# Attention, two-stage routing and a feed-forward network in one kernel: new ranks for the last blocks of attention, and more comparisons by differences

## The chip, the cores and the metric

The kernel runs on one core of a Trainium2 chip. The metric is the device time of one execution in microseconds. One execution was profiled; every row below is of it.

## The reference

Three layers follow one another. Attention over 2 x 8 heads of 768 positions (a window of 128 positions and 4 sink positions) gives a row of 512 numbers for each of 1536 tokens. A gate of 8 experts then assigns the tokens greedily, best logit first, 192 tokens to an expert, and each expert applies two products to its tokens. A last network with a sloped ReLU follows.

```
scores = np.where(is_sink | in_window, scale * q @ k.T, -1e9)
x = softmax(scores) @ v                    # 1536 x 512 after the heads are joined
logits = x @ w_gate                        # 1536 x 8
for idx in np.argsort(-logits.flatten()):  # the best logit first
    tok, e = idx // E, idx % E
    if assigned[tok] >= 0 or counts[e] >= cap: continue
    assigned[tok] = e; counts[e] += 1
out[mask_e] = maximum(x[mask_e] @ w1[e], 0) @ w2[e]
h = out @ w_in
return (maximum(h, 0) + alpha * minimum(h, 0)) @ w_out
```

## The kernel before

Attention runs over 12 blocks of 128 tokens, numbered 0 to 11 in the order of the work, each in four steps of two heads. TensorE forms scores (L459) and transposes the exponentials (L494); VectorE masks and takes minima (L469) and forms the low halves `ptl` of the transposed exponentials (L504); ScalarE takes exponentials (L480) and the high halves `pth` (L503). TensorE then weights the values (L545 to L553) into a bank `pv` of PSUM. A block fills two such banks, one for each half of its heads, and there are two of them in all, so that a block's first bank is that of the block before.

`fin` normalises one half of a block: three VectorE instructions `r` (L575), its reciprocal (L577) and `x` (L572), the last of which frees the bank. `send` stores the block's `x` and brings it to the gate: blocks 0 to 9 through a transposing DMA, blocks 10 and 11 through TensorE (L590), a high half on ScalarE (L593) and a low half on VectorE (L595), both called `xT`. The gate's product (L619) and a copy (L625) give the logits `L`. Twice, at blocks 1 and 5, VectorE also prepares the sinks' values (`vsh`, L432).

The first phase of the routing (`closing(0, ...)`) then compares each token's best logit with those of all others. It does so in two groups, blocks 0 to 8 and blocks 9 to 11: the maxima `m` of the group's tokens (L953), their row `mrow` on all partitions (TensorE L981, ScalarE L985), and for each block c1 a matrix `cm` of comparisons, whose columns TensorE counts (L1047). A comparison has two forms: directly on VectorE (L1000, from 32-bit `mrow`), or "via" a difference `minus` on ScalarE or GpSimd (L1005, L1007), of which VectorE takes the sign from 16-bit numbers (L1011 for the diagonal, L1015 for the sides). Comparisons of a block with blocks of its own group went via differences; those of blocks 0 to 8 with the 384 columns of blocks 9 to 11 went directly, nine instructions at L1000. After all counts the phase ends (L1059 on), and expert 0's tokens are gathered.

The order is set by a planner, `Plan.run`. Every `task` has an engine or a choice of two, an assumed duration, and what it reads and writes. A task's rank is the length of the longest chain behind it plus its `boost`. The planner plays the program with the assumed durations; where several tasks could start within 0.03 us on an engine, the one of highest rank goes. On the chip each engine executes its list in that order. Attention and the first phase's comparisons are planned together, the rest afterwards.

Of the kernel before, what the change touches and what calls it, by code (L numbers as in the profile page):

```python
# [212 lines left out]
OP = mybir.AluOpType  # L213
# [3 lines left out]
B, H, S, D = 2, 8, 768, 64  # L217
NB = S // 128
NBLK = B * NB
# [5 lines left out]
TURNED = 2  # L225
URGENT = 10.0
EAGER = 40.0
ORDER = "k q a b w s c d"
BY_ACT = (0, 1, 3)
BIG = 1.0e30  # L230
# [7 lines left out]
def dve(n):  # L238
    return n / 960 + 0.065
# [6 lines left out]
def attention(tc, nc, plan, ctx, qT, kT, v, vs, wg, xd, x_blocks, L, l_blocks, n_sink, window, ident, identr):  # L246
# [6 lines left out]
    task = plan.task  # L253
# [24 lines left out]
    vsh_res, sv_res = [Res() for _ in range(B)], [Res() for _ in range(B)]  # L278
# [73 lines left out]
    svf, isv = [None] * B, [None] * B  # L352
# [210 lines left out]
    def fin(t, hf):  # L563
        bank, r = PV[t, hf], r_r.new()
        b = t // NB
        if hf == 0:
            X[t] = r_x.new()
        x = X[t]
        o = lambda: bank.tile[:, 0:HC].rearrange("p (h c) -> p h c", c=D + 1)

        def scale():
            nc.vector.tensor_tensor(x.tile[:, hf * 256:(hf + 1) * 256].rearrange("p (h d) -> p h d", h=4), o()[:, :, 0:D],  # L572
                                    r.tile.unsqueeze(2).to_broadcast([128, 4, D]), OP.mult)

        task({"DVE": 0.13}, lambda: nc.vector.tensor_scalar(r.tile, o()[:, :, D], 1.0e-9, svf[b], OP.add, OP.mult),  # L575
             r=[bank.part("o"), sv_res[b]], w=[r])
        task({"DVE": 0.1}, lambda: nc.vector.reciprocal(r.tile, r.tile), w=[r])  # L577
        task({"DVE": dve(256)}, scale, r=[bank.part("o"), r], w=[x.part(hf)])

    def send(t):  # L580
        b, x = t // NB, X[t]
        parts = [x.part(0), x.part(1)]
        task({"SP": 0.06}, lambda: nc.sync.dma_start(out=xd[block(t) * 128:(block(t) + 1) * 128, :], in_=x.tile), r=parts,
             w=[x_blocks[t]], nbytes=1 << 18)
        if t >= NBLK - TURNED:
            pt, xT = r_pt.new(), r_xT.new()

            def turn():
                for c in range(NP):
                    nc.tensor.transpose(pt.tile[:, c], x.tile[:, c * 128:(c + 1) * 128], ident)  # L590

            pe(0.5, turn, parts, [pt])
            task({"ACT": act(DM)}, lambda: nc.scalar.activation(xT.tile[:, 0], pt.tile, AF.Copy, scale=svf[b]),  # L593
                 r=[pt, sv_res[b]], w=[xT.part(0)])
            task({"DVE": dve(DM) + 0.065}, lambda: nc.vector.scalar_tensor_tensor(  # L595
                xT.tile[:, 1], pt.tile, svf[b], xT.tile[:, 0], OP.mult, OP.subtract), r=[pt, sv_res[b], xT.part(0)],
                w=[xT.part(1)])
            XT[t] = xT
            return
        x16, xs, xT = r_x16.new(), r_xs.new(), r_xT.new()  # L600
        task({"ACT": 0.613}, lambda: nc.scalar.activation(x16.tile[:, 0], x.tile, AF.Copy, scale=svf[b]),
             r=[*parts, sv_res[b]], w=[x16.part(0)])
        task({"POOL": 0.67}, lambda: nc.gpsimd.tensor_scalar(xs.tile, x.tile, svf[b], 0.0, OP.mult, OP.add),
             r=[*parts, sv_res[b]], w=[xs])
        task({"POOL": 1.12}, lambda: nc.gpsimd.tensor_tensor(x16.tile[:, 1], xs.tile, x16.tile[:, 0], OP.subtract),
             r=[xs, x16.part(0)], w=[x16.part(1)])
# [230 lines left out]
class Routed:  # L837
# [94 lines left out]
    def closing(self, s, st, groups, r_bank, hold=(), fetched=False):  # L932
# [15 lines left out]
        for a, b in groups:  # L948
# [41 lines left out]
            for a1, b1 in done:  # L990
                for c1 in range(a1, b1):
                    cm, cut = self.r_cm.new(), []
                    at = c1 * 128
# [21 lines left out]
                        nc.vector.tensor_scalar(d, d, 0.0, None, OP.is_gt if op is OP.is_lt else OP.is_ge)  # L1015

                    lo = 0 if a1 == a else a
                    via = a1 == a and (c1 * 7 % 12) < self.VIA[s]
                    rr = [m.part(a1), *(rows if a1 == a else fresh)]
                    if a1 == a:  # L1020
                        sides = ((0, at, at + 128, None), (1, 0, at, OP.is_lt), (2, at + 128, b * 128, OP.is_le))
                    else:
                        sides = ((2, a * 128, b * 128, OP.is_le),)
                    if via:
                        for x, y, kk in ((0, at + 128, (0, 1)), (at + 128, b * 128, (2,))):
                            if y > x:
                                n = y - x
                                seq.append(task({"ACT": act_sb(n), "POOL": n * 1.0e-3 + 0.02},
                                                lambda e, x=x, y=y, f=minus: f(e, x, y), r=rr, bias=self.EVEN,
                                                w=[cm.part(k) for k in kk if k != 1 or at]))  # L1030
# [571 lines left out]
```

## Time and profile before

| | |
|---|---|
| median of 3 runs | 682.1 us (680.96 to 685.27) |
| time of the profiled execution | 686.03 us |
| its span, first to last instruction | 684.3 us |

The span and the time of the profiled execution differ by 1.7 us, which lies around the instructions. The profiled execution is 3.9 us above the median of the three runs. A span of one execution is thus to be compared with that of another, and the median with a median.

### The profile page before, as it was taken

Reading aid. Unit: us, or ns where it says so; the run is one execution under the profiler, and the core shown is the slowest. Engines: PE = TensorE matmul, PEld = TensorE weight load, DVE = VectorE, ACT = ScalarE, POOL = GpSimd, SP = SyncE. Lnnn points to the kernel's source line nnn. Section 1 sums busy time; section 2 is a strip of 40 time slices with the busy share of each in tenths; the row PEclk is TensorE's granted clock in tenths of the full one; section 3 lists DMA queues with packets and bytes.
Section 4 is the critical chain, followed back from the end, with each engine's and each line's share of the span. In section 5 each row is a group of like instructions: output and inputs, shape, how many; then the busy total and the mean of one; then the engine's idle time right before and its main releaser. Section 6 shows DMA issues by size and latency. Waiting matters only on the chain.

```text
span 684.3 us, 12642 instructions
## 1 busy us (share of the span) xinstructions
PE 605.0 (88%) x4490; PEld 519.1 (76%) x4491; DVE 505.5 (74%) x1203; ACT 394.6 (58%) x835; POOL 399.2 (58%) x415
## 2 busy tenths in 40 slices
PE   6789994789789695998899999989899999999996
PEld 3566773479788584778888878788798888889995
DVE  6799989789499899797888577777845556874430
ACT  6588896254474556246774344467555447766552
POOL 4766735344354477267766565667556556766663
PEclk9999996589899898799999999999999999999999
DMA  7756332536773444025610004257000326610001
GB/s 241 225 142 138 94 94 83 188 113 227 253 276 97 165 138 147 1 63 181 201 65 2 2 24 139 62 185 233 23 0 1 116 61 185 200 33 1 0 1 46
DMA packets 40283, 76.10 MB, mean 111 GB/s; under 512 B 15518, under 2 KB 22204, under 8 KB 40124
## 3 DMA queue, kind: packets, MB, share of 16 engines
q1 hardware_dynamic: 37916, 68.45, 32.6%
q0 software_dynamic: 2304, 6.84, 2.9%
q8 instruction: 35, 0.57, 0.3%
q14 instruction: 28, 0.23, 0.1%
HBM read 66.30 MB, written 6.36 MB: 106 GB/s over the span
## 4 chain that ended last, share of the span: by engine, by line
PE 49%; DVE 28%; issue 7%; DMA 7%; ACT 5%; POOL 3%; SPq 1%; POOLq 0%; DVEq 0%; ACTq 0%
PE h L1453 15%; PE o L1474 14%; DVE cm L1000 4%; PE s L459 4%; PE h L1378 3%; PE pt L494 3%; DVE ohs L1147 2%; DVE w L799 2%; DVE spl L1321 2%; DMA raw<-w 2%; PE h L1385 2%; PE r L1296 2%; ACT spl L1330 2%; DMA xg<-xd,sidx 2%; POOL spl L1321 2%
## 5 line engine op out<-in xcount | busy, mean ns | idle before, releaser
L1321 POOL TENSOR_TENSOR spl<-w,spl 128x512 fp32r<-128x512 f32 x106 | 141.3, 1335 | 98.4 <-ACT spl L1330 96.2
L1474 PE MATMUL o<-spl,gt 128*128 128x512 f32 x576 | 152.6, 407 | 1.0 <-POOL gt L1321 1.0
L1453 PE MATMUL h<-x,spl 128*128 128x384 f32 x768 | 149.7, 345 | 1.3 <-POOL x L1321 0.7
L1453 PEld LDWEIGHTS h<-x,spl 128*128 128x128 f32 x768 | 138.7, 193 | 6.7 <-DVE x L1321 1.1
L1474 PEld LDWEIGHTS o<-spl,gt 128*128 128x128 f32 x576 | 107.0, 193 | 21.1 <-POOL gt L1321 1.9
L1321 POOL TENSOR_TENSOR spl<-raw,spl 128x512 fp32r<-128x512 f32 x57 | 75.8, 1336 | 36.7 <-ACT spl L1330 27.5
L1330 ACT CAST spl<-w 128x512 fp32r<-128x512 f32 x128 | 78.6, 615 | 29.4 <-PE o L1474 22.2
L1459 DVE SCALAR_TENSOR_TENSOR v<-h,way,t 128x384 f32<-128x384 f32 x64 | 39.0, 611 | 58.6 <-ACT t L1457 58.4
L1457 ACT ACTIVATE t<-h,slope 128x384 f32<-128x384 f32 x64 | 37.0, 579 | 73.1 <-PE h L1453 73.1
L1378 PE MATMUL h<-xT,spl 128*128 128x384 f32 x192 | 59.0, 372 | 8.8 <-DVE jt L1366 8.8
L1330 ACT CAST spl<-raw 128x512 fp32r<-128x512 f32 x94 | 56.4, 619 | 16.8 <-PE o L1474 10.4
L1378 PE MATMUL h<-h,spl 128*128 128x384 f32 x192 | 56.1, 362 | 2.5 <-DVE jt L1366 2.5
L1461 ACT CAST gt<-v 128x384 fp32r<-128x384 f32 x64 | 32.8, 513 | 39.2 <-DVE v L1459 37.7
L1321 DVE TENSOR_TENSOR gt<-v,gt 128x384 fp32r<-128x384 f32 x41 | 38.6, 942 | 20.3 <-ACT gt L1461 20.3
L1047 PEld LDWEIGHTS <-cm 128*128 128x128 bf16 x684 | 24.2, 99 | 37.8 <-DVE cm L1000 27.7
L1000 DVE TENSOR_SCALAR cm<-mrow,m 128x384 bf16<-128x384 f32 (+10 forms) x85 | 51.9, 647 | 1.1 <-ACT mrow L985 1.1
L1321 DVE TENSOR_TENSOR spl<-raw,spl 128x512 fp32r<-128x512 f32 x39 | 40.7, 1050 | 14.4 <-ACT spl L1330 14.2
L1380 PE MATMUL h<-xT,spl 128*128 128x192 f32 x192 | 48.8, 254 | 0.0
L480 ACT ACTIVATE P<-sm,mn 128x260 f32<-128x260 f32 (+1 forms) x96 | 43.2, 490 | 9.6 <-DVE mn L469 8.7
L1380 PE MATMUL h<-h,spl 128*128 128x192 f32 x192 | 48.1, 251 | 0.0
L1378 PEld LDWEIGHTS h<-xT,spl 128*128 128x128 f32 x192 | 37.0, 193 | 11.7 <-DVE jt L1366 10.3
L806 POOL TENSOR_TENSOR w<-w,sg 128x512 f32<-128x512 f32 x18 | 22.2, 1234 | 39.4 <-DVE w L799 26.2
(219 smaller groups left out, 1307.8 us busy)
## 6 DMA issues: line engine op xcount, KB each, us to landing
raw<-w SPq DMA_DIRECT2D x64, 512.0 KB, 3.9
r<-w_in SPq DMA_DIRECT2D x16, 512.0 KB, 3.6
r<-w_out SPq DMA_DIRECT2D x16, 512.0 KB, 4.0
vraw<-v SPq DMA_DIRECT2D x4, 768.0 KB, 11.6
xd<-x SPq DMA_DIRECT2D x12, 256.0 KB, 2.0
k<-kT SPq DMA_DIRECT2D x11, 260.0 KB, 5.4
q<-qT SPq DMA_DIRECT2D x11, 256.0 KB, 2.8
mrow<-md SPq DMA_DIRECT2D x3, 384.0 KB
```

What stands on the lines that cost most here:

```text
L459: nc.tensor.matmul(s.tile[:, :n], lhsT=qs[t].tile[half, p], rhs=kk, start=True, stop=True)
L480: task({"ACT": act(n) + 0.137}, lambda h=h, sm=sm, mn=mn: nc.scalar.activation(P[t].tile[:, h, :n], sm.tile[:, :n], AF.Exp, bias=mn.tile, ...
L1000: nc.vector.tensor_scalar(cm.tile[:, x:y], mrow[:, x:y], m.tile[:, c1:c1 + 1], None, op)
L1321: eng.tensor_tensor(*aps(), OP.subtract)
L1330: (nc.scalar.copy if e == "ACT" else nc.vector.tensor_copy)(b.tile[:, 0], get())
L1378: nc.tensor.matmul(ps.tile[:, 0:2 * CAP], lhsT=w[:, 0, k], rhs=x.rearrange("p a t -> p (a t)"), start=first and k == 0, stop=False, skip_g ...
L1380: nc.tensor.matmul(ps.tile[:, CAP:2 * CAP], lhsT=w[:, 1, k], rhs=x[:, 0], start=False, stop=last and k == len(xs) - 1, skip_group_check=True)
L1453: nc.tensor.matmul(ps.tile[:, 0:CH], lhsT=w[:, i, k], rhs=x[:, j], start=(k == n == 0), stop=(k == KD - 1 and n == 2))
L1457: task({"ACT": act(CH)}, lambda: nc.scalar.activation(t.tile, ps.tile[:, 0:CH], AF.Copy, scale=slope), r=[ps, weights.way_res], w=[t])
L1459: task({"DVE": dve(CH) + 0.065}, lambda: nc.vector.scalar_tensor_tensor(v.tile, ps.tile[:, 0:CH], way, t.tile, OP.mult, OP.max), r=[ps, t, ...
L1461: task({"ACT": act_sb(CH)}, lambda: nc.scalar.copy(gt.tile[:, 0], v.tile), r=[v], w=[gt.part(0)])
L1474: nc.tensor.matmul(ops[t].tile, lhsT=gt.tile[:, i, sl], rhs=wo.tile[:, j], start=(f == n == 0), stop=(f == FB - 1 and n == 2))
```

## The change

Three things change. The three instructions of `fin` get longer assumed durations (0.2, 0.17 and 0.42 in place of 0.13, 0.1 and 0.33), in all blocks. In the last three blocks `fin` gets a boost of 40, as do the two halves `xT` of blocks 10 and 11. And of the nine comparisons of blocks 0 to 8 with blocks 9 to 11, those with c1 % 3 other than 2 (six of them) go via differences.

```diff
+LAST = 3
@@ fin
+        up = EAGER if t >= NBLK - LAST else 0.0
-        task({"DVE": 0.13}, lambda: nc.vector.tensor_scalar(r.tile, o()[:, :, D], 1.0e-9, svf[b], OP.add, OP.mult),
-             r=[bank.part("o"), sv_res[b]], w=[r])
-        task({"DVE": 0.1}, lambda: nc.vector.reciprocal(r.tile, r.tile), w=[r])
-        task({"DVE": dve(256)}, scale, r=[bank.part("o"), r], w=[x.part(hf)])
+        task({"DVE": 0.2}, lambda: nc.vector.tensor_scalar(r.tile, o()[:, :, D], 1.0e-9, svf[b], OP.add, OP.mult),
+             r=[bank.part("o"), sv_res[b]], w=[r], boost=up)
+        task({"DVE": 0.17}, lambda: nc.vector.reciprocal(r.tile, r.tile), w=[r], boost=up)
+        task({"DVE": 0.42}, scale, r=[bank.part("o"), r], w=[x.part(hf)], boost=up)
@@ send
-                 r=[pt, sv_res[b]], w=[xT.part(0)])
+                 r=[pt, sv_res[b]], w=[xT.part(0)], boost=EAGER)
-                w=[xT.part(1)])
+                w=[xT.part(1)], boost=EAGER)
@@ closing
-                    via = a1 == a and (c1 * 7 % 12) < self.VIA[s]
+                    via = (a1 == a or c1 % 3 != 2) and (c1 * 7 % 12) < self.VIA[s]
-                        for x, y, kk in ((0, at + 128, (0, 1)), (at + 128, b * 128, (2,))):
+                        for x, y, kk in ((0, at + 128, (0, 1)), (at + 128, b * 128, (2,))) if a1 == a else (
+                                (a * 128, b * 128, (2,)),):
```

The lines of the changed kernel stand one to three further down (L572 becomes L573, L595 L597, L1000 L1002, L1007 L1009, L1015 L1017). All instructions keep their number but for these six comparisons, each of which becomes a difference and a sign. From the end of the first phase on, every engine's order is the one of before.

The first place is VectorE at block 11, where the block's two halves `x` stand among the comparisons of the first group. Before:

```order
L572 TENSOR_TENSOR x_2357<-pv_2296,r_2346 128x256
L1015 TENSOR_SCALAR cm_2317<-cm_2317 128x1024
L504 TENSOR_TENSOR ptl_2367<-pt_2342,pth_2359 128x256
L595 SCALAR_TENSOR_TENSOR xT_2363<-pt_2307,scv_163,xT_2363 128x512
L575 TENSOR_SCALAR r_2392<-pv_2348,scv_163 128x4
L1015 TENSOR_SCALAR cm_2331<-cm_2331 128x896
L577 RECIPROCAL r_2392<-r_2392 128x4
L1011 TENSOR_TENSOR cm_2361<-cm_2361,trih 128x128
L572 TENSOR_TENSOR x_2357<-pv_2348,r_2392 128x256
```

After, at the same place:

```order
L573 TENSOR_TENSOR x_2347<-pv_2294,r_2322 128x256
L577 TENSOR_SCALAR r_2357<-pv_2339,scv_163 128x4
L1017 TENSOR_SCALAR cm_2324<-cm_2324 128x1024
L579 RECIPROCAL r_2357<-r_2357 128x4
L597 SCALAR_TENSOR_TENSOR xT_2355<-pt_2330,scv_163,xT_2355 128x512
L573 TENSOR_TENSOR x_2347<-pv_2339,r_2357 128x256
L1013 TENSOR_TENSOR cm_2327<-cm_2327,trih 128x128
L1017 TENSOR_SCALAR cm_2327<-cm_2327 128x128
L1017 TENSOR_SCALAR cm_2327<-cm_2327 128x896
```

The second half of block 11 now leaves ahead of four signs that stood before it (two diagonals, 128 and 896 columns). Its `xT`, further on, and the maxima of the second group have the same place in VectorE's list as before, behind the same comparisons.

The second place is the second group, on GpSimd. Before, its differences after the last three of the first group:

```order
L1007 TENSOR_SCALAR cm_2433<-mrow,m_2265 128x256
L1007 TENSOR_SCALAR cm_2438<-mrow,m_2265 128x1024
L1007 TENSOR_SCALAR cm_2467<-mrow,m_2265 128x1152
L1007 TENSOR_SCALAR cm_2555<-mrow,m_2265 128x256
L1007 TENSOR_SCALAR cm_2560<-mrow,m_2265 128x1408
L1283 DMA xg_2819<-xd,sidx_2812 128x512
```

After:

```order
L1009 TENSOR_SCALAR cm_2423<-mrow,m_2252 128x256
L1009 TENSOR_SCALAR cm_2436<-mrow,m_2252 128x1024
L1009 TENSOR_SCALAR cm_2436<-mrow,m_2252 128x128
L1009 TENSOR_SCALAR cm_2557<-mrow,m_2252 128x384
L1009 TENSOR_SCALAR cm_2565<-mrow,m_2252 128x384
L1009 TENSOR_SCALAR cm_2573<-mrow,m_2252 128x384
L1009 TENSOR_SCALAR cm_2583<-mrow,m_2252 128x256
L1009 TENSOR_SCALAR cm_2595<-mrow,m_2252 128x1408
L1286 DMA xg_2825<-xd,sidx_2818 128x512
```

Three differences of 384 columns are new at the head of the second group; the other three stand on ScalarE, also ahead of its own. In the first group GpSimd gives up the differences of 768 and 1152 columns to ScalarE and takes one of 512 and two of 128. VectorE's own list for the second group is now:

```order
L1002 TENSOR_SCALAR cm_2559<-mrow,m_2252 128x384
L1002 TENSOR_SCALAR cm_2563<-mrow,m_2252 128x384
L1017 TENSOR_SCALAR cm_2555<-cm_2555 128x384
L1017 TENSOR_SCALAR cm_2557<-cm_2557 128x384
L1017 TENSOR_SCALAR cm_2561<-cm_2561 128x384
L1017 TENSOR_SCALAR cm_2565<-cm_2565 128x384
L1017 TENSOR_SCALAR cm_2571<-cm_2571 128x384
L1017 TENSOR_SCALAR cm_2573<-cm_2573 128x384
L1002 TENSOR_SCALAR cm_2600<-mrow,m_2252 128x384
L1017 TENSOR_SCALAR cm_2583<-cm_2583 128x256
```

Before, nine rows of L1000 stood in place of the first nine; the eight signs of blocks 9 to 11 follow them in both.

The third place is VectorE at the end of block 5, one of the blocks of attention that only the new durations move. Before:

```order
L575 TENSOR_SCALAR r_1396<-pv_1249,scv_157 128x4
L432 SCALAR_TENSOR_TENSOR vsh<-vsr,scv_163,vsh 32x16x64
L577 RECIPROCAL r_1396<-r_1396 128x4
L575 TENSOR_SCALAR r_1426<-pv_1350,scv_157 128x4
L572 TENSOR_TENSOR x_1430<-pv_1249,r_1396 128x256
L577 RECIPROCAL r_1426<-r_1426 128x4
L504 TENSOR_TENSOR ptl_1433<-pt_1370,pth_1404 128x512
L572 TENSOR_TENSOR x_1430<-pv_1350,r_1426 128x256
```

After:

```order
L577 TENSOR_SCALAR r_1406<-pv_1251,scv_157 128x4
L577 TENSOR_SCALAR r_1412<-pv_1340,scv_157 128x4
L579 RECIPROCAL r_1406<-r_1406 128x4
L579 RECIPROCAL r_1412<-r_1412 128x4
L433 SCALAR_TENSOR_TENSOR vsh<-vsr,scv_163,vsh 32x16x64
L573 TENSOR_TENSOR x_1435<-pv_1251,r_1406 128x256
L573 TENSOR_TENSOR x_1435<-pv_1340,r_1412 128x256
L505 TENSOR_TENSOR ptl_1453<-pt_1368,pth_1414 128x512
```

The two halves of the block now stand side by side, so that the first half's `x` comes behind the second half's `r`. In blocks 0 to 9 of the changed kernel nearly all halves stand so; before, those of blocks 0, 1, 2 and 4 did.

## Rows read from the trace of the kernel before

**Rows 1.** The page: busy time, share of the span and instructions of each engine.

```profile
PE 605.0 (88%) x4490; PEld 519.1 (76%) x4491; DVE 505.5 (74%) x1203; ACT 394.6 (58%) x835; POOL 399.2 (58%) x415
```

**Rows 2.** Busy time by stage: attention, first group, second group.

```profile
40.00:100.00 60.00, 57.44 (x807) 43.34 (x807) 55.96 (x228) 53.28 (x128) 36.08 (x63) 1.00 0.47 113
99.76:113.53 13.77, 8.24 (x156) 6.87 (x153) 13.07 (x45) 9.12 (x20) 8.28 (x10) 0.79 0.26 62
113.53:122.60 9.07, 4.71 (x77) 3.37 (x75) 7.23 (x23) 4.72 (x6) 2.21 (x2) 0.50 0.35 117
```

**Rows 3.** Timelines of VectorE and ScalarE, first group: start, duration, instruction.

```profile
102.57 0.86 DVE L1011 TENSOR_TENSOR cm<-cm,trih 128x128 bf16<-128x128 bf16 x1
...
107.89 1.05 DVE L1011 TENSOR_TENSOR cm<-cm,trih 128x128 bf16<-128x128 bf16 x1
108.87 0.27 DVE L1015 TENSOR_SCALAR cm<-cm 128x384 bf16<-128x384 bf16 x1
109.06 1.27 DVE L1015 TENSOR_SCALAR cm<-cm 128x640 bf16<-128x640 bf16 x1
110.25 0.20 DVE L1011 TENSOR_TENSOR cm<-cm,trih 128x128 bf16<-128x128 bf16 x1
...
110.92 0.31 DVE L1015 TENSOR_SCALAR cm<-cm 128x640 bf16<-128x640 bf16 x1
111.15 0.74 DVE L595 SCALAR_TENSOR_TENSOR xT<-pt,scv,xT 128x512 f16<-128x512 f32 x1
111.81 0.24 DVE L1015 TENSOR_SCALAR cm<-cm 128x384 bf16<-128x384 bf16 x1
111.98 0.21 DVE L1011 TENSOR_TENSOR cm<-cm,trih 128x128 bf16<-128x128 bf16 x1
...
112.41 0.27 ACT L625 ACTIVATE L<-pv,scv 128x8 f32<-128x8 f32 x1 [3.23 <-PE pv L619]
```

**Rows 4.** GpSimd's differences of the first group: the last, and means by shape.

```profile
108.86 1.29 POOL L1007 TENSOR_SCALAR cm<-mrow,m 128x1152 bf16<-128x1152 f32 x1
L1007 POOL TENSOR_SCALAR cm<-mrow,m 128x384 bf16<-128x384 f32 x2 | 1.3, 668 | 0.0
L1007 POOL TENSOR_SCALAR cm<-mrow,m 128x768 bf16<-128x768 f32 x1 | 0.9, 901 | 0.0
L1007 POOL TENSOR_SCALAR cm<-mrow,m 128x512 bf16<-128x512 f32 x1 | 0.7, 687 | 0.0
```

**Rows 5.** Timeline of the second group, VectorE, GpSimd and ScalarE.

```profile
115.42 2.49 DVE L1000 TENSOR_SCALAR cm<-mrow,m 128x384 bf16<-128x384 f32 x3 [1.09 <-ACT mrow L985]
116.32 3.56 DVE L1000 TENSOR_SCALAR cm<-mrow,m 128x384 bf16<-128x384 f32 x7
119.80 0.21 DVE L1011 TENSOR_TENSOR cm<-cm,trih 128x128 bf16<-128x128 bf16 x1
121.22 0.51 DVE L1015 TENSOR_SCALAR cm<-cm 128x1408 bf16<-128x1408 bf16 x1
122.37 0.26 DVE L1059 SCALAR_TENSOR_TENSOR both<-s,far 128x96 f32<-128x96 f32 x1 [0.65 <-PE s L1047]
115.49 2.21 POOL L1007 TENSOR_SCALAR cm<-mrow,m 128x256 bf16<-128x256 f32 x2 [5.34 <-ACT mrow L985]
115.42 3.12 ACT L1005 ACTIVATE cm<-mrow,m 128x1280 bf16<-128x1280 f32 x3
```

**Rows 6.** Line L1000, comparisons of the second group: least, median, longest ns.

```profile
L1000 DVE TENSOR_SCALAR cm<-mrow,m x9: 402/407/1589, 115.4 to 119.5; 128x384 bf16<-128x384 f32 x9
```

**Rows 7.** TensorE's and VectorE's timelines at the ends of blocks 1, 4 and 5.

```profile
38.95 0.19 PE L545 MATMUL pv<-vh,pth 128*128 128x65 f16 x1 [1.28 <-DVE x L572]
68.77 0.19 PE L545 MATMUL pv<-vh,pth 128*128 128x65 f16 x1 [0.69 <-DVE x L572]
59.60 0.76 DVE L572 TENSOR_TENSOR x<-pv,r 128x256 f32<-128x256 f32 x2
66.52 1.28 DVE L432 SCALAR_TENSOR_TENSOR vsh<-vsr,scv,vsh 32x1024 f16<-32x1024 f32 x1
```

## The prediction

> **What bounds the kernel now.** I read the page first, then the busy times by stage, then the timelines of the stages that the change touches. On the page TensorE is busy for 605.0 us (88% of the span) and VectorE for 505.5 us [rows 1]. That average says little here, since all that is moved lies ahead of 122.6 us; behind it every engine's order is the one of before, and I take a shift of the first phase's end to pass through one to one. The busy times by stage [rows 2] show what bounds the three stages concerned. In attention (40 to 100 us) TensorE is busy for 57.44 of 60 us, VectorE for 55.96: TensorE sets the pace, and VectorE has some 4 us to spare. In the first group of comparisons, from one maximum to the next (99.76 to 113.53), VectorE is busy for 13.07 of 13.77 us: VectorE is the bound. In the second group it is busy for 7.23 of 9.07 us, with a wait for `mrow` of 1.09 us ahead of the comparisons and one for the counts of 0.65 us behind them [rows 5].
>
> Busy is not the same as working, though. The timeline of the first group has a diagonal of 128 columns that takes 1.05 us and another that takes 0.86, where the next one takes 0.20, and a sign of 640 columns that takes 1.27 us where a later one of the same size takes 0.31 [rows 3]. The long ones end right behind a difference on GpSimd: its last difference of the group begins, and so the one ahead of it ends, at 108.86, and the diagonal of 1.05 us ends at 108.94; the last difference ends at 110.15, and the 1.27 us sign at 110.33 [rows 3, 4]. So these VectorE instructions stand still while GpSimd forms a difference, and get through when one ends and the next begins. In the second group, three direct comparisons span 2.49 us and end at 117.91, GpSimd's two differences end at 117.70, and the last six then need 119.88 - 117.91 = 1.97 us, 0.33 us each [rows 5]; the longest took 1.589 us where the median is 0.407 [rows 6].
>
> **The change part by part.**
>
> First group. VectorE's list from one maximum to the next has the same instructions but for one `x` and a reciprocal (0.34 + 0.09 us), which now come behind the first maximum and not ahead of it; that moves the maximum forward by as much and costs nothing in all. What can be gained is the standing still. The three long rows alone lose (1.05 - 0.20) + (0.86 - 0.20) + (1.27 - 0.31) = 2.5 us [rows 3]. GpSimd's list gets shorter: it loses 768 columns (0.90) and 1152 columns (1.29 us) and gains 512 (0.69) and two of 128, which have no row; one of 384 takes 0.67, so that two of 128 lie between 0 and 1.34 us, and I take 0.5 for both by the shape's size [rows 4]. That is -0.90 - 1.29 + 0.69 + 0.5 = -1.0 us, and GpSimd is through at some 109.2 instead of 110.15. VectorE's 640-column sign would be released that much sooner, and all behind it, which then runs unhindered [rows 3], moves up: -1.0 us at the second maximum. It still needs block 11's logits; these were there at 112.68, 0.8 us behind the end of `xT` at 111.89 [rows 3], and `xT` moves up as well, since the second half of `x` leaves four signs earlier. Bounds: -2.5 us if none of the three stands still, +0.5 us if the longer list of differences on ScalarE (1152 columns more in sum, most of it behind the last `xT`) holds `xT` up. I take -1.0. The boost of `xT` itself is priced at nothing: it has the place in VectorE's list that it had.
>
> Second group. VectorE loses six direct comparisons of 0.33 us and gains six signs of 384 columns, each 111.98 - 111.81 = 0.17 us [rows 3, 5]: -0.96 us if nothing stands still. But GpSimd gets three differences of 384 columns more, 3 x 0.67 = 2.0 us [rows 4], ahead of its two that took 2.21 us, and is through at about 119.7 instead of 117.70. Until then VectorE gets through only at the ends of GpSimd's instructions, at about 116.2, 116.8, 117.5, 118.2 and 119.7. At 108.86 a diagonal and a sign of 384 columns passed together and a third instruction had to wait [rows 3]; of the longer 0.33 us comparisons one passed at an end [rows 5]. With two short ones at an end, the two direct comparisons pass at 115.4 and 116.2 and the six signs at 116.8, 117.5 and 118.2. At 119.7 what is left is one direct comparison (0.33) and the eight signs of blocks 9 to 11, which took 121.73 - 119.80 = 1.93 us: 121.96 and some overlap, against 121.73 before. With one at an end it is 0.34 us more. ScalarE's three differences more are 1152 columns, where its own three of 2944 took 3.12 us: by columns 1.2 us, and with something for each start 1.5 us, so that its last ends at about 120.0 instead of 118.54 [rows 5], while VectorE asks for it at about 121.4: covered. I take +0.2 us, with -0.96 - 1.4 = -2.4 as the lower bound (nothing stands still: three comparisons took 2.49 us where 3 x 0.33 and the last one's tail need 1.07), and +0.6 as the upper by these rows.
>
> A rule of the Trainium skill bears on this. SBUF — State Buffer, section "Who interferes with whom", says that VectorE's faster modes and GpSimd share a pair of ports, and that whichever starts first keeps it for a whole instruction while the other fully blocks. The rows agree as to the whole instruction; that one or two VectorE instructions pass at each end, the rule doesn't say. [...]
>
> Attention. The new durations make the planner put a block's two halves side by side. TensorE's first weighting product of the next block needs the first half's bank, which the first half's `x` frees. Where VectorE was late with it, TensorE waited 1.28 us (block 1) and 0.69 us (block 5) [rows 7]. At both ends `vsh` (1.28 us) stands in front of `x`. At block 4 the halves stood side by side already, without `vsh`, and no wait of TensorE over 0.2 us follows the pair at 59.60 [rows 7]. So side by side alone costs nothing there; TensorE has scores and transposes to do in between. In the changed order `vsh` of block 5 stands behind the second half's reciprocal, so the first bank comes free somewhat later: I take +0.4 us for the whole stage. Bounds: -2 us, if both waits go; +5.5 us, if each of some 8 blocks more waits as block 5 did (8 x 0.69).
>
> Sum: -1.0 + 0.2 + 0.4 = -0.4 us. The profiled execution would take 686.03 - 0.4 = 685.6 us; that one lies 3.9 us above the median of its kernel, which is what is predicted: 682.1 - 0.4 = 681.7 us.
>
> **The rivals.**
>
> The bank is held (slower). One mechanism: halves side by side hold the first bank until the second half is weighed, in every block. For it: the two waits [rows 7] and TensorE's pace, which lets any such wait through to the end. Against it: block 4. Price 0.69 us to 1.28 us for each of 8 blocks, 5.5 to 10.2 us, less 0.8 us gained elsewhere: 686.8 to 691.5 us. It decides from 0.1 us a block on, and makes the kernel slower by over 1% from 0.95 us a block.
>
> No VectorE instruction passes until GpSimd's list of the second group is through at 119.7: then eight comparisons (2 x 0.33 + 6 x 0.17 = 1.68) and 1.93 us follow, 123.3 instead of 121.73, or +1.6 us; with -1.0 in the first group and +0.4 in attention, 683.1 us. Against it: two instructions passed at 108.86 [rows 3]. [...]
>
> The change does not do what it says: the last `xT` is where it was, VectorE's queue and not the rank decides, and the second maximum stays put because other instructions stand still in place of those. Then 0 + 0.2 + 0.4, 682.7 us.
>
> Most of the standing still goes: half of the lower bounds of all three stages together, (-2.5 - 2.4 - 2) / 2 = -3.5, 678.6 us; all of them, 675.2 us. For it: GpSimd's list no longer meets the signs at the same moments. Against it: in the second group there is more GpSimd work, not less.
>
> **How the numbers follow.** The forecast of 681.7 us gets 0.42, the list that nothing passes 0.13, the change without effect 0.20, the gain of standing still 0.15, the held bank 0.10. About 1% (6.8 us) is what a measurement of this kernel can tell from no change. The first three lie within 1%; of the gain rival I give 0.05 to over 1% and of the bank 0.06; for what I overlooked, 0.01 on each side. Faster by over 1%: 0.06; slower by over 1%: 0.07; within: 0.87. The range holds the first three, most of the gain rival and the lower end of the held bank: 677.0 to 687.0 us.
>
> **What the profile after would show.** If the steps are right: from one maximum to the next on VectorE some 12.8 us instead of 13.77; GpSimd through with the first group about 1 us sooner after the first maximum; in the second group, from the first comparison to the last sign, 6.3 to 6.9 us (6.31 before), with single signs of 384 columns that take 0.5 us and more; ScalarE's last difference not waited for; TensorE's waits on `x` at blocks 1 and 5 of about 1 us, and none over 0.3 us at the others. The forecast would be wrong if TensorE waited for `x` at every block, if signs in the second group ran at 0.17 us each despite GpSimd, or if the stages behind 122.6 us changed in length although their order is the same.

## The result, and the profile after

The changed kernel is slower: its median is 691.4 us over 20 runs, beside 687.5 us for the kernel before over as many. The medians differ by 3.9 us; the ratio is 1.0074, 95% interval 1.0054 to 1.0095, which is 5.1 us (3.7 to 6.5). A ratio leaves out the runs of a kernel that lie over 1.5% above its fastest, and for both exchanges, `L` ahead alone, both with early old and the boosted first half (the experiments below) that takes away 8 of the 26 runs of before, so that the medians of all runs would give only 1.0026, 1.0069, 1.0007 and 1.0004 there. (The three runs of before that are shown ahead, with a median of 682.1 us, were from the lower part of its spread of 680.96 to 691.48 us.) The profiled execution took 689.76 us with a span of 688.1 us, beside 686.03 and 684.3 us.

The page of the changed kernel, busy times and the clock granted to TensorE in 40 slices:

```profile
PE 607.2 (88%) x4490; PEld 519.1 (75%) x4491; DVE 505.9 (74%) x1203; ACT 397.2 (58%) x837; POOL 401.2 (58%) x419
...
PEclk9989998569899898699999999999999999999999
```

The busy times are those of [rows 1], to 3 us. The time went into waits, and the windows that answer to [rows 2] say where:

```profile
40.00:100.00 60.00, 55.11 (x705) 39.74 (x703) 50.32 (x192) 47.28 (x112) 34.20 (x60) 0.95 0.44 101
106.20:119.09 12.89, 8.22 (x169) 7.28 (x165) 12.40 (x45) 10.18 (x20) 8.96 (x13) 0.80 0.33 86
119.09:128.12 9.03, 4.48 (x77) 3.38 (x75) 7.19 (x23) 6.25 (x9) 4.16 (x5) 0.50 0.36 119
```

In attention TensorE does 705 products in the 60 us in which it did 807, at a granted clock of 0.95 in place of 1.00. The two groups of comparisons are as long as forecast. VectorE's timeline of the changed kernel at the two maxima, the second group and the phase's end, and GpSimd's of the second group:

```profile
106.20 0.22 DVE L955 TENSOR_REDUCE m<-L 128x9 f32<-128x72 f32 x1
119.09 0.16 DVE L955 TENSOR_REDUCE m<-L 128x3 f32<-128x24 f32 x1
120.98 1.09 DVE L1002 TENSOR_SCALAR cm<-mrow,m 128x384 bf16<-128x384 f32 x2 [1.10 <-ACT mrow L987]
121.99 1.91 DVE L1017 TENSOR_SCALAR cm<-cm 128x384 bf16<-128x384 bf16 x6
123.83 1.60 DVE L1002 TENSOR_SCALAR cm<-mrow,m 128x384 bf16<-128x384 f32 x1
127.91 0.26 DVE L1062 SCALAR_TENSOR_TENSOR both<-s,far 128x96 f32<-128x96 f32 x1 [0.64 <-PE s L1050]
...
121.05 4.16 POOL L1009 TENSOR_SCALAR cm<-mrow,m 128x384 bf16<-128x384 f32 x5 [4.97 <-ACT mrow L987]
```

The first maximum comes at 106.20 in place of 99.76 (+6.44), the second 12.89 us behind it in place of 13.77 (-0.88), and from the first comparison to `both` it is 6.93 us in place of 122.37 - 115.42 = 6.95 [rows 5]. So the phase ends 5.54 us late, and all of it lies ahead of the first maximum, in attention.

Where in attention, the end of each block's second `x` tells (start plus duration of its row). From one block's end to the next, in us:

| block | 2 | 3 | 4 | 5 | 6 | 7 | 8 | 9 |
|---|---|---|---|---|---|---|---|---|
| before | 7.62 | 9.22 | 4.28 | 9.35 | 6.92 | 6.98 | 7.78 | 5.05 |
| after | 10.42 | 7.62 | 8.30 | 8.45 | 7.62 | 7.62 | 7.62 | 9.06 |

Against before, block 2 loses 2.80 us, blocks 3 to 5 lose 1.52, blocks 6 to 8 lose 1.18. From the end of block 8 to the second maximum it is 22.76 us in place of 22.14 (+0.62); block 1 itself ended 0.55 us sooner. With -0.02 for the second group that is the 5.54, to 0.01.

**Block 2.** VectorE's and TensorE's timelines of the changed kernel at the end of block 1:

```profile
34.28 0.64 DVE L401 TENSOR_SCALAR wg<-wgs,scw 128x32 f16<-128x32 f32 x1
34.95 0.69 DVE L402 SCALAR_TENSOR_TENSOR wg<-wgs,scw,wg 128x32 f16<-128x32 f32 x1
35.57 0.23 DVE L579 RECIPROCAL r<-r 128x4 f32<-128x4 f32 x2
35.83 2.06 DVE L433 SCALAR_TENSOR_TENSOR vsh<-vsr,scv,vsh 32x1024 f16<-32x1024 f32 x1
37.92 0.76 DVE L573 TENSOR_TENSOR x<-pv,r 128x256 f32<-128x256 f32 x2
...
38.40 0.19 PE L546 MATMUL pv<-vh,pth 128*128 128x65 f16 x1 [3.02 <-DVE x L573]
```

TensorE now waits 3.02 us for `x`, where it waited 1.28 [rows 7]. The same three instructions stood ahead of `x` before, but were shorter. VectorE and GpSimd of the kernel before, same place:

```profile
36.14 0.23 DVE L400 TENSOR_SCALAR wg<-wgs,scw 128x32 f16<-128x32 f32 x1
36.41 0.25 DVE L401 SCALAR_TENSOR_TENSOR wg<-wgs,scw,wg 128x32 f16<-128x32 f32 x1
...
36.95 1.28 DVE L432 SCALAR_TENSOR_TENSOR vsh<-vsr,scv,vsh 32x1024 f16<-32x1024 f32 x1
...
37.24 1.55 POOL L421 TENSOR_SCALAR vraw<-vraw,scv 128x512 f32<-128x512 f32 x1
```

GpSimd of the changed kernel:

```profile
34.11 0.70 POOL L420 TENSOR_SCALAR vh<-vraw,scv 128x512 f16<-128x512 f32 x1
...
34.91 0.70 POOL L422 TENSOR_SCALAR vraw<-vraw,scv 128x512 f32<-128x512 f32 x1
35.69 1.12 POOL L424 TENSOR_TENSOR vl<-vraw,vh 128x512 f16<-128x512 f32 x1
```

Before, `vsh` started first and GpSimd's `vraw` took 1.55 us; after, GpSimd started first each time and VectorE's three took 0.64, 0.69 and 2.06 us, 1.63 us more than before, which is nearly the 1.74 us by which TensorE's wait grew. The loser is the one that TensorE waits for.

Behind the wait the clock falls. Windows of the 8 us behind it, after and before:

```profile
38.40:46.40 8.00, 7.80 (x73) 5.74 (x72) 5.20 (x21) 5.09 (x11) 2.51 (x5) 0.57 0.48 134
```

```profile
38.95:46.95 8.00, 7.78 (x119) 5.85 (x118) 7.28 (x30) 6.80 (x16) 4.99 (x10) 1.00 0.51 134
```

Both are busy for 7.8 us, but the one with 73 products and the other with 119: after 3.02 us of idling TensorE is granted 0.57 on average, near the lower of its two levels (1.2 and 2.4 GHz); after 1.28 us it kept 1.00.

**The later blocks.** TensorE's waits from 60 to 100 us (releaser, sum in us, times, longest), before and then after:

```profile
PE pv L545 <- DVE x L572: 0.7, 1, 0.7
PE pv L619 <- DMA xT<-x: 0.5, 1, 0.5
PE pt L494 <- DVE r L577: 0.4, 1, 0.4
```

```profile
PE pt L495 <- DVE ptl L505: 2.1, 5, 0.6
PE pv L546 <- DVE x L573: 1.0, 1, 1.0
```

So it is `ptl` that TensorE waits for at block after block, not the first bank. VectorE's timeline at the end of block 7 of the changed kernel, and TensorE's and ScalarE's:

```profile
87.01 0.22 DVE L577 TENSOR_SCALAR r<-pv,scv 128x4 f32<-128x4 f32 x1 [0.30 <-PE pv L554]
...
87.41 0.42 DVE L573 TENSOR_TENSOR x<-pv,r 128x256 f32<-128x256 f32 x1
88.29 0.42 DVE L573 TENSOR_TENSOR x<-pv,r 128x256 f32<-128x256 f32 x1 [0.46 <-PE pv L523]
88.63 0.68 DVE L505 TENSOR_TENSOR ptl<-pt,pth 128x512 f16<-128x512 f32 x1
...
85.09 0.66 PE L495 MATMUL pt<-ident,P 128*128 128x128 f32 x4
...
88.09 0.19 PE L546 MATMUL pv<-vh,pth 128*128 128x65 f16 x1
...
89.46 0.41 PE L495 MATMUL pt<-ident,P 128*128 128x128 f32 x2 [0.37 <-DVE ptl L505]
...
88.91 0.72 ACT L603 ACTIVATE x<-x,scv 128x512 f16<-128x512 f32 x1
89.53 0.25 ACT L627 ACTIVATE L<-pv,scv 128x8 f32<-128x8 f32 x1
```

This `ptl` belongs to the transposes of 85.09. It stands in VectorE's list behind the second half's `r`, which waits 0.30 us for the block's last product, and behind the second half's `x`, which waits 0.46 us for TensorE's transposed sinks (L523), written into the same bank. TensorE's next transposes need the buffer that `ptl` frees. On ScalarE the logits' copy `L` stands behind the high half of `x` (L603), and TensorE's next weighting product goes into the bank that `L` reads.

VectorE's timeline of the kernel before, at the end of block 6:

```profile
75.10 0.21 DVE L575 TENSOR_SCALAR r<-pv,scv 128x4 f32<-128x4 f32 x1
75.22 0.41 DVE L572 TENSOR_TENSOR x<-pv,r 128x256 f32<-128x256 f32 x1
...
75.64 0.66 DVE L504 TENSOR_TENSOR ptl<-pt,pth 128x512 f16<-128x512 f32 x1
76.22 0.41 DVE L572 TENSOR_TENSOR x<-pv,r 128x256 f32<-128x256 f32 x1
```

Here too the first half's `x` comes behind the second half's `r`, and so it does at blocks 5 and 7, beside the blocks 0, 1, 2 and 4 named ahead. What differs at blocks 6 and 7 is that a `ptl` stands between the two `x`; "apart" means no more than that there.

### The profile page after: what moved, and what is told of

Read it like the earlier page. It is cut to its first block, busy times and chain, and to the rows that moved or that the text cites. A ratio compares the mean times of both kernels' runs of the same rounds, so it can differ in the third digit from the quotient of the medians.

```text
span 688.1 us, 12645 instructions
## 1 busy us (share of the span) xinstructions
PE 607.2 (88%) x4490; PEld 519.1 (75%) x4491; DVE 505.9 (74%) x1203; ACT 397.2 (58%) x837; POOL 401.2 (58%) x419
## 4 chain that ended last, share of the span: by engine, by line
PE 40%; DVE 27%; issue 6%; DMA 4%; ACT 4%; POOL 2%; POOLq 0%; DVEq 0%; ACTq 0%; SPq 0%
PE o L1477 14%; PE h L1456 14%; DVE cm L1002 4%; PE h L1381 4%; DVE ohs L1150 3%; DVE w L801 2%; PE h L1388 2%; DMA raw<-w 2%; DVE spl L1324 2%; PE r L1299 2%; PE h L1383 2%; ACT spl L1333 2%; DMA xg<-xd,sidx 2%; DVE h L1373 2%; DVE cm L1017 1%
## 5 line engine op out<-in xcount | busy, mean ns | idle before, releaser
L1477 PE MATMUL o<-spl,gt 128*128 128x512 f32 x576 | 154.7, 411 | 0.7 <-POOL gt L1324 0.6
L1002 DVE TENSOR_SCALAR cm<-mrow,m 128x384 bf16<-128x384 f32 (+10 forms) x79 | 51.1, 679 | 1.1 <-ACT mrow L987 1.1
```

The lines of the kernel that those rows point to most:

```text
L1002: nc.vector.tensor_scalar(cm.tile[:, x:y], mrow[:, x:y], m.tile[:, c1:c1 + 1], None, op)
L1477: nc.tensor.matmul(ops[t].tile, lhsT=gt.tile[:, i, sl], rhs=wo.tile[:, j], start=(f == n == 0), stop=(f == FB - 1 and n == 2))
```

## The experiments

All times are compared with the kernel before, run on the same chip; the trace's numbers are in a table at the end of this section.

**The parts of the change.** The first two separate the durations from the rest. The first is the kernel before with the durations alone, the second the changed kernel without them:

```diff
-        task({"DVE": 0.13}, lambda: nc.vector.tensor_scalar(r.tile, o()[:, :, D], 1.0e-9, svf[b], OP.add, OP.mult),
-        task({"DVE": 0.1}, lambda: nc.vector.reciprocal(r.tile, r.tile), w=[r])
-        task({"DVE": dve(256)}, scale, r=[bank.part("o"), r], w=[x.part(hf)])
+        task({"DVE": 0.2}, lambda: nc.vector.tensor_scalar(r.tile, o()[:, :, D], 1.0e-9, svf[b], OP.add, OP.mult),
+        task({"DVE": 0.17}, lambda: nc.vector.reciprocal(r.tile, r.tile), w=[r])
+        task({"DVE": 0.42}, scale, r=[bank.part("o"), r], w=[x.part(hf)])
```

> The kernel before with the longer assumed durations in fin alone: no boost, no more differences. If the durations make the loss: the first maximum of the first phase comes about 6.4 us later than in the kernel before (106.2 against 99.76), TensorE waits some 3 us for x at the end of block 1 and runs at about 0.55 of its clock behind that, the first group takes 13.8 us as before, and the time is some 6 us (ratio 1.009) above that of the kernel before. If the boosts or the six new differences make it: ratio 1.000 and no such wait.

Measured: 1.0122 (1.008 to 1.0164). The first maximum came at 106.76, with a wait of 3.1 us at block 1; the clock behind it was 0.79, not 0.55.

> The changed kernel with the old assumed durations; the boosts and the six new differences stay. If the durations make the loss: first maximum within 0.5 us of 99.76, a granted clock of 1.00 from 40 to 100 us, the first group some 12.9 us instead of 13.77, the second as before, and a ratio of 0.998 to 0.999. If the boosts make it: first maximum some 6 us late and a ratio of 1.007.

Measured: 1.0023 (0.9992 to 1.0055). From the end of block 1 the phase ended 82.15 us later (before 83.14, after 89.23). The first maximum missed its forecast, at 101.21, with the second only 10.18 us behind it: its moment alone tells little, and the end of the phase is what I go by. The intervals of the two runs don't meet: the longer durations make the loss. That the boosts and differences gain anything in time is not shown; 1.0 us less in the trace stands against a ratio whose interval reaches from a gain of 0.5 to a loss of 3.8 us.

**Which blocks.** My theory at this point was that the wait at block 1 and the clock behind it were most of the loss.

```diff
-        task({"DVE": 0.42}, scale, r=[bank.part("o"), r], w=[x.part(hf)], boost=up)
+        task({"DVE": 0.42 if t < 2 else dve(256)}, scale, r=[bank.part("o"), r], w=[x.part(hf)], boost=up)
```

The other two durations go alike; the second run has t >= 2 in place of t < 2.

> The changed kernel with the longer durations in blocks 0 and 1 alone; there vsh of the first batch stands between the reciprocals and x of block 1, and from block 2 on the order is that of the old durations. If the one wait at block 1 and the clock behind it are most of the loss: wait of some 3 us at the end of block 1, granted clock of about 0.55 for some 8 us, first maximum some 4.5 us late, ratio 1.005. If the loss is the bank that is held in every later block: first maximum at most 1 us late, ratio 0.999 to 1.001.

Measured: 1.0033 (1.0004 to 1.0062); wait 3.0 us, clock 0.57 behind it, block 2 in 10.55 us.

> The changed kernel with the longer durations from block 2 on; blocks 0 and 1 have the order of the old ones, with vsh ahead of the reciprocals. If the wait at block 1 and the clock behind it are most of the loss: wait at block 1 of about 1.3 us, granted clock of 1.00 from 40 to 100 us, first maximum some 2 us late, ratio 1.001 to 1.002. If the bank that is held in every later block is the cause: first maximum some 6 us late, blocks of 7.6 us and more, ratio 1.007.

Measured: 1.0063 (1.0031 to 1.0094); wait 1.3 us at block 1, blocks 6 to 8 of 7.63, 7.63 and 7.62 us. The theory fell: the later blocks alone lose as well, more than the 1.001 to 1.002 that it gave; which of the two parts is the larger, the ratios don't show (their intervals meet). Against the kernel with the old durations the trace has 6.3 us more for the later blocks and 3.3 for the early ones; both together (the changed kernel) 7.1, so they don't add up. With a late block 2 TensorE waits 1.2 us at block 4 for the transposing DMA of `x`, and its clock stays at 1.00 behind that; without it, 1.7 us, and the clock falls:

```profile
57.60:65.60 8.00, 8.00 (x83) 5.64 (x84) 4.67 (x20) 5.24 (x12) 3.16 (x8) 0.79 0.44 103
```

So the 6.3 us hold a stretch at block 4 (10.29 us) that the changed kernel (8.30) does not have.

**Which queue.** The next three move single neighbours. First, `ptl` goes ahead of the second half's `x` on VectorE, seven rows of its list; all other engines' lists stay:

```diff
+        def low():
+            nc.vector.tensor_tensor(view(lo, nk), view(pt, nk), view(hi, nk), OP.subtract)
+            while held:
+                held.pop()()
+        task({"DVE": dve(256 * nk)}, low, r=[pt, hi], w=[lo])
...
-        task({"DVE": 0.42}, scale, r=[bank.part("o"), r], w=[x.part(hf)], boost=up)
+        task({"DVE": 0.42}, (lambda: held.append(scale)) if hf and 2 <= t <= 8 else scale,
+             r=[bank.part("o"), r], w=[x.part(hf)], boost=up)
```

> The changed kernel with one pair of neighbours exchanged in VectorE's list of each of blocks 2 to 8: ptl goes ahead of the second half's x. Every other engine's order is the same. Theory: in the changed kernel the second half's x waits for a product of TensorE (the transposed sinks, which share its bank) with ptl queued behind it, and TensorE then waits 0.56 us a block for ptl. Then the blocks take about 7.1 us in place of 7.62, TensorE's waits for ptl of 0.4 to 0.6 us go, the first maximum comes some 3.5 us sooner behind the end of block 1 and the ratio to the kernel before is 1.002 to 1.003. Rival, the bank of the first half is held too long: the exchange leaves the first half's x where it is, so blocks stay at 7.6 us and the ratio at 1.006 to 1.008.

Measured: 1.0123 (1.0066 to 1.018). The waits for `ptl` went, and blocks 6 to 8 still took 7.41, 7.58 and 7.93 us. TensorE's waits from 60 to 100 us of this run (its lines stand four further down):

```profile
PE pv L550 <- ACT L L631: 2.1, 4, 0.7
PE pv L550 <- DVE x L577: 1.0, 1, 1.0
```

Another wait has taken the place: for ScalarE's `L`. The mirror image is the same exchange on ScalarE, `L` ahead of the high half of `x`, once with the one on VectorE and once alone:

```diff
+        def copy():
+            nc.scalar.activation(L[:, t], lg(), AF.Copy, scale=isv[t // NB])
+            while kept:
+                kept.pop()()
+        task({"ACT": 0.17}, copy, r=[w, sv_res[t // NB]], w=[l_blocks[t]], boost=URGENT)
...
+        def high():
+            nc.scalar.activation(x16.tile[:, 0], x.tile, AF.Copy, scale=svf[b])
+        task({"ACT": 0.613}, (lambda: kept.append(high)) if 2 <= t <= 8 else high,
+             r=[*parts, sv_res[b]], w=[x16.part(0)])
```

> The changed kernel with ScalarE's exchange alone (L ahead of the high half of x, blocks 2 to 8). If the two queues stand in a row: ptl is still late, TensorE still waits 0.4 to 0.6 us a block for it, blocks 7.6 us, ratio 1.006 to 1.008. If L were the only cause: blocks of 7.1 us, ratio 1.003.

Measured: 1.0129 (1.0073 to 1.0186); blocks 6 to 8 of 7.62, 7.63 and 7.62 us.

> The changed kernel with two pairs of neighbours exchanged at blocks 2 to 8: on VectorE ptl ahead of the second half's x, and on ScalarE the logits' copy L ahead of the block's high half of x (16 bits). TensorE's and GpSimd's order is that of the changed kernel. Theory: two queues in a row delay TensorE at the end of a block, ptl behind x on VectorE and L behind the high half on ScalarE, and with the first alone removed the second took its place (0.48 us a block in the run with ptl ahead of x). Then blocks take 6.9 to 7.1 us in place of 7.6, TensorE's waits for ptl and for L both go, and the ratio is 1.002 to 1.004 (the wait at block 1 stays). Rival: it is TensorE's own order (scores in lots of four, not of eight) that sets the pace; then blocks stay at 7.4 to 7.6 us with yet another wait.

Measured: 1.0074 (1.0037 to 1.0112), beside the 1.0129 of the ScalarE exchange alone on the same chip. Waits from 60 to 100 us, of the ScalarE exchange alone and then of both:

```profile
PE pt L495 <- DVE ptl L505: 1.7, 4, 0.6
PE pv L546 <- DVE x L573: 1.0, 1, 1.0
```

```profile
PE pv L550 <- DVE x L577: 1.1, 1, 1.1
PE pv L628 <- DMA xT<-x: 0.6, 1, 0.6
PE pt L495 <- PE s L460: 0.2, 1, 0.2
```

With both, the waits for `ptl` and for `L` are gone, and blocks 3, 6 and 7 take 6.99, 6.74 and 7.07 us in place of 7.62. TensorE's order is that of the changed kernel, so that rival falls for these blocks. But blocks 4 and 5 take 8.61 us each (8.30 and 8.45 in the changed kernel), with a wait for the transposing DMA of 1.5 us at block 4, and block 8 takes 8.07. Over blocks 6 to 8 the two exchanges give back 0.98 of the 1.18 us lost, over blocks 3 to 5 only 0.16 of 1.52: what makes that loss stays open. In time the gain over the changed kernel, 2.4 us in the trace (0.74 of it in block 2, ahead of the exchanges), is not shown, nor is one over `L` ahead alone: the intervals overlap, and the ratio of 1.002 to 1.004 that I expected was missed.

> The kernel with the longer durations from block 2 on, with both pairs of neighbours exchanged at blocks 2 to 8. No wait of 3 us at block 1, and, if the two queues are the cause, blocks of 6.9 to 7.1 us: first maximum within 1 us of the kernel with the old durations, ratio 0.999 to 1.002. If TensorE's own order sets the pace: as the run with durations from block 2 on, 1.006.

Measured: 1.0033 (0.9998 to 1.0068): blocks 6 and 7 in 6.74 and 7.06 us, no long wait at block 1, but block 4 in 10.27 with a wait of 1.6 us for the transposing DMA and a clock of 0.79 behind it. The ratio expected, at most 1.002, was missed; against the later blocks alone (1.0063) the intervals meet.

**`vsh`.** Two runs move it behind `x`:

```diff
@@ prep_vs
-        task({"DVE": 1.15}, lambda: nc.vector.scalar_tensor_tensor(
+        task({"DVE": 1.15}, lambda: late.append(lambda: nc.vector.scalar_tensor_tensor(
@@ scale, in fin, behind x
+            while hf and late:
+                late.pop()()
```

> As the run with ptl ahead of x, and vsh (blocks 1 and 5) behind both halves' x in VectorE's list. TensorE's wait of 3 us at the end of block 1 falls below 1 us and the granted clock stays at 1.00 behind it; block 2 ends some 8 us behind block 1 in place of 10.4. If a wait at that place counts in the end: 2 to 3 us faster than the run with ptl ahead of x alone, ratio 0.998 to 1.000. If it is given back behind the first phase, as the run with the longer durations in blocks 0 and 1 suggests (first maximum 4 us later than with the old durations, time only 0.6 us more): within 1 us of that run.

Measured: 1.0114 (1.0077 to 1.015). The wait for `x` fell to 0.96 us, but `ptl` now stood behind `vsh` and TensorE waited 1.7 us for it; the clock in the 8 us behind that was 0.79, not the 1.00 that I expected, block 2 took 10.62 us, and block 6, at the second `vsh`, 10.16 in place of 7.41.

> The kernel before with vsh behind both halves' x in VectorE's list at blocks 1 and 5, nothing else moved. TensorE's waits of 1.28 and 0.69 us for x go. If nothing takes their place: 2 us faster, ratio 0.997. If ptl, which then stands behind vsh at block 1, is late in place of x: ratio 0.999 to 1.001 and a wait for ptl of about 1 us there.

Measured: 1.0052 (1.0019 to 1.0086), slower. TensorE's and VectorE's timelines of this run at block 1:

```profile
40.01 0.63 PE L494 MATMUL pt<-ident,P 128*128 128x128 f32 x4 [1.80 <-DVE ptl L504]
...
37.88 1.28 DVE L432 SCALAR_TENSOR_TENSOR vsh<-vsr,scv,vsh 32x1024 f16<-32x1024 f32 x1
39.17 0.69 DVE L504 TENSOR_TENSOR ptl<-pt,pth 128x512 f16<-128x512 f32 x1
```

The rival held, and at a higher price than it gave: 1.80 us for `ptl` in place of 1.28 for `x`. In the 8 us behind it the clock was 0.79 in place of 1.00, and block 2 took 10.59 us in place of 7.62.

**The rest.** The differences alone, in the kernel before (the columns of a difference change with this line, as in the change):

```diff
-                    via = a1 == a and (c1 * 7 % 12) < self.VIA[s]
+                    via = (a1 == a or c1 % 3 != 2) and (c1 * 7 % 12) < self.VIA[s]
```

> The kernel before with the six new differences alone; attention's order is that of before. Second group from the first comparison to the end of the phase some 6.9 to 7.2 us (6.95 before), first group 13.8 us as before since the boosts moved its x; ratio 1.000. If GpSimd's three differences more let no VectorE instruction pass: second group 8.5 us, ratio 1.002.

Measured: 1.0008 (0.9975 to 1.0041); the first group 13.80 us (before 13.77), and from the second maximum to `both` 8.82 us (before 8.84).

And an order with the halves apart in spite of the longer durations:

```diff
-        up = EAGER if t >= NBLK - LAST else 0.0
+        up = EAGER if not hf or t >= NBLK - LAST else 0.0
```

> The changed kernel with the boost of 40 on the first half's three instructions in every block. The planner then sends the halves apart in most blocks, as before the change, with the longer durations; vsh no longer stands between a reciprocal and x. If the order side by side is the cause: blocks of about 7.0 us, no wait over 1.3 us for x, first maximum as in the kernel before or up to 2 us sooner, ratio 0.997 to 1.001. If the longer durations harm in another way: ratio 1.006.

Measured: 1.0025 (0.9986 to 1.0065), no difference from the kernel before, though its profiled span, 680.4 us, is the shortest of all; nor is one from the changed kernel shown, whose interval this one meets. Blocks of 7.0 us came only in part: blocks 3 to 5 took 24.71 us together. In the trace (84.31 us to `both`, with the longer durations in every block, in place of 89.23) it is the order that costs, as it must be: an assumed duration reaches the chip only through the order.

From the end of block 1 to the end of the phase, and three stretches of it (us, from the ends of `x` and the start of `both`):

| kernel | block 2 | 3 to 5 | 6 to 8 | to `both` | ratio |
|---|---|---|---|---|---|
| before | 7.62 | 22.85 | 21.68 | 83.14 | 1 |
| after | 10.42 | 24.37 | 22.86 | 89.23 | 1.0074 |
| durations alone | 9.16 | 24.16 | 22.75 | 88.61 | 1.0122 |
| old durations | 7.63 | 22.34 | 21.68 | 82.15 | 1.0023 |
| blocks 0, 1 | 10.55 | 22.67 | 21.68 | 85.40 | 1.0033 |
| blocks 2 to 11 | 7.62 | 26.37 | 22.88 | 88.42 | 1.0063 |
| `ptl` ahead | 10.37 | 24.69 | 22.92 | 89.50 | 1.0123 |
| `L` ahead | 9.14 | 24.36 | 22.87 | 87.97 | 1.0129 |
| both ahead | 9.68 | 24.21 | 21.88 | 86.81 | 1.0074 |
| both, early old | 7.62 | 25.78 | 21.48 | 85.87 | 1.0033 |
| and `vsh` behind | 10.62 | 23.92 | 25.67 | 91.71 | 1.0114 |
| before, `vsh` behind | 10.59 | 22.67 | 23.33 | 87.57 | 1.0052 |
| differences alone | 7.62 | 22.47 | 21.68 | 82.76 | 1.0008 |
| first half boosted | 7.01 | 24.71 | 21.32 | 84.31 | 1.0025 |

## Why the prediction was wrong

The forecast of 681.7 us missed by its third term. Of the 9.7 us between it and the median of 691.4 us, 5.4 are the base, a median of three runs that lay 5.4 us below that of all 20; with an exact -0.4 us it would have been 687.1 us. Against the 20 runs it is -0.4 us forecast and +5.1 us measured by the ratio (+3.9 by the medians).

- **First group, -1.0 us:** near in the number, half right in the steps. The stretch fell by 0.88 us. GpSimd is through 9.88 us behind the first maximum in place of 10.39, 0.51 us sooner and not 1.0; the rest came behind the end of its list (3.01 us to the second maximum in place of 3.38), where I had priced nothing. From the end of block 8 to the second maximum it is 23.70 us with the durations alone and 22.76 in the changed kernel, so the boosts and differences give 0.94 us there; with the old durations only 0.47 (21.67 in place of 22.14).
- **Second group, +0.2 us:** right, -0.02. The picture of two short signs at each end of a GpSimd difference held: the six signs took 1.91 us, 0.24 us for the first of a pair and 0.46 to 0.56 for the second, where they would have needed 1.0 us at 0.17 each. The direct comparison behind them took 1.60 us, until 125.43; GpSimd's list ended at 125.21. The rival in which nothing passes falls (its 1.6 us were not there). The Trainium skill, SBUF — State Buffer, section "Who interferes with whom", says that of VectorE in its two-port modes and GpSimd whoever issues first holds the shared ports for a whole instruction and blocks the other. The trace agrees as to whole instructions (the 1.60 us of the direct comparison; `vraw` and `vsh` above, 1.55 and 2.06 us). That a list without gaps keeps VectorE out altogether, the page does not say, and here it did not.
- **Attention, +0.4 us:** the step that failed. "So side by side alone costs nothing there; TensorE has scores and transposes to do in between." The first maximum came 6.44 us later, beyond the upper bound of 5.5. The runs showed three parts in place of the +0.4: 2.80 us in block 2 (next point); 1.18 us over blocks 6 to 8 (0.70, 0.64 and -0.16), by two queues in a row, of which both exchanges together give back 0.98; and 1.52 us over blocks 3 to 5, of which they give back 0.16. The cause of this last part stays open; what shows there is a wait of 1.18 us for the transposing DMA at block 4. (From the end of block 8 to the first maximum it is 9.87 us in place of 8.37, most of which is back at the second maximum.) The rival "the bank is held" (8 blocks of 0.69 us) came near in size by luck and had the mechanism wrong: at block 7 the first half's `x` ends at 87.83 and the next block's first product starts at 88.09, without a wait, and at blocks 6 and 7 of the kernel before the first half's `x` already came behind the second half's `r`. What is held up is what stands behind the pair on VectorE (`ptl`) and on ScalarE (`L`). At blocks 1 and 5, with `vsh`, TensorE did wait for the first half's `x`.
- **The same term, at block 1:** I had both bounds from waits of 1.28 and 0.69 us and took `vsh` at 1.28 us. That GpSimd's work would start ahead of it, and make it 2.06 us, no list tells (GpSimd's own is the same there, from `sk` to `vl`), but the kernel before had the two overlapping, with `vraw` the slower, and I priced no other outcome; that TensorE's clock falls behind 3 us of idling, nothing in this stage of the trace before told. I expected waits of about 1 us at blocks 1 and 5 and none over 0.3 us elsewhere; there were 3.02 and 1.01, and five of up to 0.56 for `ptl` from 60 to 100 us.
- **Block 4 as a witness:** I looked for a wait behind one pair and found none over 0.2 us. But in the kernel before the halves stood side by side at block 2 as well, and there the trace has the very picture of the later blocks, VectorE's second `x` and then TensorE's next transposes:

```profile
46.43 0.42 DVE L572 TENSOR_TENSOR x<-pv,r 128x256 f32<-128x256 f32 x1 [0.52 <-PE pv L522]
...
47.60 0.63 PE L494 MATMUL pt<-ident,P 128*128 128x128 f32 x4 [0.54 <-DVE ptl L504]
```

Block 4 was the wrong one to ask: the chain of work that ended last goes there through a transposing DMA (58.55 to 63.30 us), for which TensorE then waits 0.51 us. That the price stood in the distances between the ends (9.22 + 4.28 + 9.35 = 22.85 us for blocks 3 to 5, beside 6.92 and 6.98) is not shown, since that DMA and the wait at block 5 lie in them.
- **A shift of the phase's end passes to the end:** held roughly. The table's "to `both`" follows the ratios within some 2 us, except for the durations alone (5.5 us in the trace, 8.4 by the ratio), `L` ahead (4.8 and 8.9) and the old durations (-1.0 and +1.6). How much of the 3 us at block 1 reaches the end stays open: with and without it the ratios are 1.0033 and 1.0023, and 1.0074 and 1.0033, with intervals that meet.

## What to carry to other kernels

To price a new order, don't look for a wait behind the pair of instructions that moved: measure the period of the loop, look at every place where the new order already stands and not at one, and in the new order follow what stands behind each moved instruction on its own engine, for every engine. When a wait vanishes and the time doesn't, look at once for the wait that took its place; here two exchanges that each gave nothing gave 0.5 to 0.9 us together in each of three blocks of six, while the other three grew by 0.2 to 0.5 us. An assumed duration that is nearer to the truth is no better in itself; what matters is the order that a planner makes of it.

## What the hardware showed unexpectedly

The same wait was followed by different clocks. In six profiles TensorE waited 3.0 to 3.1 us at the end of block 1. The windows of the 8 us behind it, with the durations alone and with both neighbours exchanged:

```profile
40.15:48.15 8.00, 7.78 (x90) 5.62 (x89) 6.03 (x25) 5.97 (x13) 2.91 (x6) 0.79 0.48 134
```

```profile
37.82:45.82 8.00, 8.00 (x86) 6.06 (x85) 5.76 (x22) 5.68 (x13) 2.51 (x5) 0.65 0.48 134
```

The lists are the same there up to the exchanges. The granted clock was 0.57 in three of the six (block 2 in 10.37 to 10.55 us), 0.65 in one (9.68) and 0.79 in two (9.14 and 9.16); in the kernel before, behind 1.28 us, it was 1.00 (7.62). Shorter waits were followed by a lower clock too: 1.62, 1.74 and 1.80 us (both with early old, blocks 2 to 11, before with `vsh` behind) by 0.79 over the next 8 us. So up to 1.4 us of block 2 is the clock and not the wait, and that part differs between executions whose wait is the same; what decides it was not found. Behind the first phase, where the order is the same in all kernels, such dips come and go too: from 490 to 500 us the granted clock was 0.83 in the profile of before and 1.00 in that of after, with the same 8.48 us of busy time (the same work lies some 4 to 6 us later there, and from 495.5 to 505.5 us the clock was 1.00 as well). That the span of the profile after is only 3.8 us longer, with a phase that ends 5.54 us later, has dips like this one in it, so single profiles shouldn't be compared to better than some 2 us there.
